# Anchors of a decay scan in one PSUM bank, early logits copied to SBUF, and a small product moved amid the value products: an attention and mixture-of-experts kernel on one core

## The chip, the cores and the metric

The kernel runs on one core of a Trainium2 chip. Five engines work side by side, each in its own order: TensorE (PE, matrix products), VectorE (DVE), ScalarE (ACT), GpSimd (POOL) and SyncE (SP), which here issues most of the transfers. Data lie in SBUF; PE writes to PSUM, which has eight banks of 512 float32 numbers for each of 128 partitions. The metric is the device time of one execution in microseconds, smaller being better.

## The reference

Three stages follow each other. The first is a linear attention with a decaying state, for 2 batches of 8 heads, 768 steps and 48 channels per head:

```python
for t in range(S):
    kt, vt, rt, wt = k[:, :, t], v[:, :, t], r[:, :, t], w[:, :, t]
    cur = einsum('bhd,bhe->bhde', u[None] * kt, vt)
    y[:, :, t] = einsum('bhd,bhde->bhe', rt, state + cur)
    state = wt[..., None] * state + einsum('bhd,bhe->bhde', kt, vt)
```

Its result, as 1536 tokens of 384 channels, goes through a mixture of 8 experts (the best expert by `x @ w_gate`, a capacity per expert, two matrices with a ReLU between them, the result scaled by the softmax weight), and then through a gated block with three matrices, `(silu(x @ w_gate) * (x @ w_val)) @ w_out`.

## The kernel before

The recurrence is done in 12 chunks of 128 steps, all heads at once. A chunk is split into two halves of 64 steps. The scan X (`prep1`, L369) forms the running products of the decay w in each half; `anchored` (L377) takes the reciprocals of X at every eighth step, the anchors; the scan R (`prep2`, L415) multiplies on from the anchors, step by step, with wm, which is w but zero where a group of eight begins (ACT fills wm in `prep0`, L406 and L407). X and R scale keys and queries: the products M (L421, L424). The data of a chunk come in as dm. The anchors stand in an SBUF tile anch of 526 columns, zero except for the 64 anchors; there are two such tiles, for even and odd chunks. `check` (L386) lets ACT sum up X and the anchors of a chunk, for a test of their size at the end.

PE then forms the products of a chunk: `scores` (`psA`, L469, copied out as A by ACT and masked by POOL), `kgtok` (transposed keys, `psT`), `state` (`psP`, L509 and L513, the state carried on, which DVE scales to Sc in L519 and ACT spreads to Sb in `expand`, L527), `values` (y, L494 and L499, in four pairs of heads) and `diag` (L441), the products with u. `xrow` (L533) adds to y the values weighted by the diagonal, aV, which POOL forms in `own` (L449). `gate_t` transposes x (L547), together with the diagonal's and the gate's rows (`gate_rows`), and ACT copies both out as xT (L552). `columns` (L576) turns these rows into columns with one matmul: the logits of the chunk before last, and the diagonal of the chunk to come, which ACT copies out as a8 (L578).

The loop `for u in range(NU - 2)` runs ten passes. Pass u prepares chunk u + 2 on DVE, forms the scores of chunk u + 1 and the values of chunk u. The order of every engine is the order in which the code is written (`manual_schedule`); `warm` puts matmuls whose result nobody reads on PE. The logits are taken in groups of chunks, (0 to 3), (4 to 7), (8, 9) and (10, 11). A group has one PSUM tile, of tag "lg" (but "P" for the third), for logits, diagonal and counts. `choose` writes the steps of a group's choice of experts into a list; `tick`, called between DVE's larger operations, takes the next from it. For the first group this happens in pass 6: one of the steps, taken between the two scans of `prep2(8)` and the products, is DVE's reciprocal of sm (L586) and, with it, ACT's scaling of four chunks, xg (L591). `count` (L652) and `place` (from L658) then give the tokens their places, and `scatter` writes them out.

PSUM is full: psA has two banks (A0, A1), psY two (y), and ps1 four, by tag: "T", "xT", "P" and "lg". A tile of a tag can be written only when all who use the tile before it in that bank have finished.

Of the kernel before, what the change touches and what calls it, by code (L numbers as in the profile page):

```python
# [10 lines left out]
F32 = mybir.dt.float32  # L11
# [14 lines left out]
HC = C // 2  # L26
# [3 lines left out]
G = 8  # L30
# [12 lines left out]
def build(tc, cap, dm, tk, vt, ub, cst, wg, w1, w2, wgate, wval, wout, out):  # L43
# [254 lines left out]
    early = ExitStack()  # L298
    ep = early.enter_context(tc.tile_pool(name="ep", bufs=2, side="right"))
    dmt = [ep.tile([128, DMW], F32, name=f"dm{i}", bufs=1) for i in range(3)]  # L300
    anch = [ep.tile([128, 2 * (NP * HC + G - 1)], F32, name=f"anch{i}", bufs=1) for i in range(2)]
    wm = [ep.tile([128, 2, NP, HC], F32, name=f"wm{i}", bufs=1) for i in range(2)]
    Sb = [ac.tile([128, NP, 2 * D], F32, name=f"Sb{i}") for i in range(2)]
    ap2 = at.enter_context(tc.tile_pool(name="ap2", bufs=2))
# [1 line left out]
    psA = at.enter_context(tc.tile_pool(name="psA", bufs=1, space=PSUM))  # L306
    ps1 = at.enter_context(tc.tile_pool(name="ps1", bufs=1, space=PSUM))
    psY = at.enter_context(tc.tile_pool(name="psY", bufs=2, space=PSUM))

    vts, Xf, Xt, Mt, kgt, Sc, At, yt, xt, xgt, xgs, av, rkt, a8s, lgt = ({} for _ in range(15))  # L310

    def run(x, up):

        x = x.rearrange("p a b -> p (a b)")
        return x if up else x[:, ::-1]

    def anchors(x, h, o):

        return x[:, h, :, h * o:h * o + HC - G + 1:G]

    def halved(x, w):
        return x[:, 0:2 * NP * w].rearrange("p (h a j) -> p h a j", h=2, a=NP)
# [1 line left out]
    def each8(x, w):  # L324


        return x.rearrange("p (h z) -> p h z", h=2)[:, :, 0:NP * w].rearrange("p h (a j) -> p h a j", a=NP)[..., 0:HC:G]
# [45 lines left out]
    def anchored(u):  # L373

        if u >= NU:
            return
        nc.vector.reciprocal(out=each8(anch[u % 2], HC), in_=each8(Xf[u], XW))  # L377
        tick()

    def check(u):  # L380

        if u >= NU:
            return
        for i, t in enumerate((each8(Xf[u], XW), each8(anch[u % 2], HC))):
            j = gp.tile([128, 2, NP, HC // G], F32, tag="sum", name="sum")
            nc.scalar.activation(out=j, in_=t, func=AF.Copy, accum_out=total[:, 2 * u + i:2 * u + i + 1])  # L386

# [21 lines left out]
    def prep2(u):  # L409

        if u >= NU:
            return
        Rt = ep.tile([128, 2, NP, HC], F32, tag="R", name="R")
        for h in range(2):
            nc.vector.tensor_tensor_scan(out=run(Rt[:, h], 1 - h), data0=run(wm[u % 2][:, h], 1 - h),  # L415
                                         data1=run(halved(anch[u % 2], HC)[:, h], 1 - h),
                                         initial=0.0, op0=ALU.mult, op1=ALU.add)
            tick()
        M = Mt[u] = ap3.tile([128, NP, 4, HC], F32, tag="M", name="M")
        kr = dmt[u % 3][:, 2 * NP * XW:].rearrange("p (a s j) -> p a s j", a=NP, s=4)  # L420
        nc.vector.tensor_tensor(out=M[:, :, 0::3, :], in0=kr[:, :, 0::3, :],  # L421
                                in1=Xt[u][:, :, :, 1:1 + HC].rearrange("p h a j -> p a h j"), op=ALU.mult)
        tick()
        nc.vector.tensor_tensor(out=M[:, :, 1:3, :], in0=kr[:, :, 1:3, :],  # L424
                                in1=Rt[:, ::-1].rearrange("p h a j -> p a h j"), op=ALU.mult)
        tick()
        if u < NU - 1:
            prep3(u)
# [23 lines left out]

    def warm(n, ps=None, tag="T"):

        ps = (ps or psA).tile([128, 512], F32, tag=tag if ps else "A0", name="psW")
        x = xinit.rearrange("p h a j -> p (h a j)").bitcast(BF16)[:, 0:512]
        for _ in range(n):
            nc.tensor.matmul(ps, ones, x, start=True, stop=True)

# [101 lines left out]

    def logits_to(u):
        g = group[u]
        if g not in lgt:
            lgt[g] = ps1.tile([128, len(g), 3 * E], F32, tag="P" if g[-1] == NU - 3 else "lg", name="lg")
        return lgt[g][:, u - g[0]]
# [6 lines left out]
    def columns(u, w, q):  # L573

        to = logits_to(w)
        nc.tensor.matmul(to[:, 0:2 * E], gss.pop(u), fold[:, 0:2 * E], start=True, stop=True)  # L576
        a8s[q] = gp.tile([128, H], F32, tag="a8", name="a8")
        nc.scalar.copy(out=a8s[q], in_=to[:, E:2 * E])  # L578

# [21 lines left out]
    def choose(us, weigh=weigh):  # L601

        n = len(us)
        u0, u1 = us[0], us[-1] + 1
        lg = lgt[us][:, :, 0:E]

        def over(x):
            return x.to_broadcast([128, n, E])

        mx, ls, ex, eq, be, sm = (small(t, n, w) for t, w in (  # L610
            ("mx", 1), ("ls", E), ("ex", E), ("eq", E), ("be", 1), ("sm", 1)))

        def s2():
            nc.vector.reduce_max(out=mx, in_=lg, axis=AX.X)

        def s3():
            nc.vector.tensor_tensor(out=ls, in0=lg, in1=over(mx), op=ALU.subtract)
            nc.scalar.activation(out=ex, in_=ls, func=AF.Exp)

        def s4():  # L620
            nc.vector.scalar_tensor_tensor(out=eq, in0=ls, scalar=0.0, in1=ev.unsqueeze(1).to_broadcast([128, n, E]),
                                           op0=ALU.is_ge, op1=ALU.mult)

        bes[us] = be

        def s5():
            nc.vector.reduce_max(out=be, in_=eq, axis=AX.X)

        def s6():
            nc.vector.tensor_tensor(out=ohs[:, u0:u1, :], in0=eq, in1=over(be), op=ALU.is_equal)  # L630

        def s7():
            nc.vector.reduce_sum(out=sm, in_=ex, axis=AX.X)

        w = weigh(us, sm)
        steps.extend([s2, s3, s4, s5, s6, s7, *w[:1], lambda: [f() for f in w[1:]]])
# [10 lines left out]
    def count(us):  # L647

        u0, n = us[0] // 4 * 4, len(us)
        pc = lgt[us][:, :, 2 * E:]  # L650
        adds = [(ohacc, us[0])] * (u0 > 0) + [(ohs[:, q, :], max(us[0], q + 1)) for q in range(u0, us[-1])]
        nc.tensor.matmul(pc, tri, ohs[:, us[0]:us[-1] + 1, :], start=True, stop=False, skip_group_check=True)  # L652
        for i, (o, q) in enumerate(adds):
            m = us[-1] + 1 - q
            nc.tensor.matmul(pc[:, n - m:], ones, o.unsqueeze(1).to_broadcast([128, m, E]), start=False,
                             stop=i == len(adds) - 1, skip_group_check=True)
# [201 lines left out]
    nc.vector.memset(xinit[:, 1, :, 1:2], 1.0)  # L858
    for i in range(2):
        nc.gpsimd.memset(wm[i], 0.0)  # L860
        nc.vector.memset(anch[i], 0.0)
    nc.vector.memset(ones, 1.0)
    prep0(0)
    prep1(0)
# [14 lines left out]
    prep1(1)  # L879
    anchored(1)  # L880
    prep2(1)
    prep0(2)
    prep1(2)
    for i in range(2):
# [3 lines left out]
    for u in range(NU - 2):  # L888
        chosen, counted = ended.get(u - 2), ended.get(u - 3)
        if u:  # L890
            prep0(u + 2)
            prep1(u + 2)
        xrow(u - 1)
        state(u)
        anchored(u + 2)
        warm((7, 4)[u] if u < 2 else 3, ps1, "xT")
        scores(u + 1)
        if u:
            own(u)
        kgtok(u + 1)  # L900
        if u:
            gate_t(u - 1, (u - 2 if u > 1 else None, u + 1))
        else:
            psr = ps1.tile([128, 2 * C], F32, tag="xT", name="psr")
            gs = gp.tile([128, DM + C], F32, tag="xT", name="gs", bufs=3)
            for q in range(2):
                diag(q, psr[:, C * q:C * q + C], True)
            nc.scalar.copy(out=gs[:, 0:2 * C], in_=psr)
            gss.update((q, gs[:, C * q:C * q + C]) for q in range(2))
            warm(2, ps1, "lg")  # L910
        expand(u)
        load_dm(u + 4)
        zero(NZ)
        if counted:
            count(counted)
            place(counted)
            ready += counted
        prep2(u + 2)
        if not u:
            check(1)  # L920
            nc.vector.tensor_copy(out=tri, in_=before)
        check(u + 2)
        if u:
            values(u)
            columns(u - 1, max(u - 2, 0), u + 1)
        else:
            values(u)
            for q in range(2):
                to = logits_to(q)
                nc.tensor.matmul(to[:, 0:E], gss.pop(q), fold[:, E:2 * E], start=True, stop=True)  # L930
            a8 = gp.tile([128, 2, H], F32, tag="a82", name="a82")
            nc.scalar.copy(out=a8, in_=lgt[group[0]][:, 0:2, 0:E])
            for q in range(2):
                a8s[q] = a8[:, q, :]
            own(0)
        if chosen:
            flush()
            if u < NU - 3:
                choose(chosen)
        load_v(u + 3)  # L940
        if u >= 4:
            load_raws(u - 3)
        if u >= 5:
            fill(0.0)
        for _ in range(2):
            if ready and not steps:
                scatter(ready.pop(0))
# [613 lines left out]
```

## Time and profile before

| | |
|---|---|
| time, median of 3 runs | 469.25 us (469.13 to 470.42) |
| time of the profiled execution | 465.57 us |
| its span, first to last instruction | 463.9 us |
| PE busy | 450.2 us (97%) |
| DVE busy | 331.0 us (71%) |
| ACT busy | 238.8 us (51%) |
| POOL busy | 70.9 us (15%) |
| mean granted clock of TensorE | 0.999 |
| recurrence and choice of experts | to about 97 us |

The span lies 1.7 us below the time of its own execution. Busy time of PE is modelled at the ends of matmuls, so a busy PE is not PE at its peak. Times in rows are counted from the span's start; an instruction's line is that of the kernel before.

### The profile page before, as it was taken

The numbers are of one execution on the slowest core, as the hardware profiler recorded it, in microseconds if no ns is written. First come the engines' busy times: TensorE is split into PE (matmuls) and PEld (weight loads), VectorE is DVE, ScalarE is ACT, GpSimd is POOL, SyncE is SP. The second block draws the span as 40 slices with busy tenths as digits, with TensorE's granted clock in tenths as the row PEclk, the third lists the DMA queues.
The fourth block names the chain that finished last, engine by engine and source line by source line (L and its number), as shares of the span: only waits on it lengthen the run. The fifth ranks groups of instructions, "written<-read, shape, count | busy, mean of one in ns | idle before, by whom it ended". The sixth has DMA issues, their size and how long they took to land.

```text
span 463.9 us, 9305 instructions
## 1 busy us (share of the span) xinstructions
PE 450.2 (97%) x3565; PEld 397.8 (86%) x3576; DVE 331.0 (71%) x690; ACT 238.8 (51%) x561; POOL 70.9 (15%) x94
## 2 busy tenths in 40 slices
PE   7998999999999999999999999999999999999994
PEld 3676767889999999999988888888888888888884
DVE  8999999877887945858599876665678585434241
ACT  4556685666877866674446454544443352231120
POOL 3324355540000000000000650000000000003033
PEclk9999999999999999999999999999999999999999
DMA  7798994139999944336134455222200000001011
GB/s 247 219 290 266 314 279 163 70 103 305 378 350 361 357 171 144 91 116 199 42 101 131 75 68 70 68 68 69 68 1 0 3 0 0 1 0 69 0 70 68
DMA packets 34801, 62.57 MB, mean 135 GB/s; under 512 B 5504, under 2 KB 17280, under 8 KB 34752
## 3 DMA queue, kind: packets, MB, share of 16 engines
q1 hardware_dynamic: 32832, 57.20, 40.5%
q0 software_dynamic: 1920, 4.73, 2.8%
q8 instruction: 29, 0.48, 0.5%
q14 instruction: 20, 0.16, 0.1%
HBM read 52.48 MB, written 9.44 MB: 133 GB/s over the span
## 4 chain that ended last, share of the span: by engine, by line
PE 80%; DVE 9%; issue 4%; DMA 4%; ACT 1%; POOL 1%; POOLq 0%; SPq 0%; DVEq 0%; ACTq 0%
PE psg L1418 32%; PE psu L1441 14%; PE psh L1297 14%; PE pso L1315 13%; DMA dm<-in_dm 2%; DVE R L415 2%; DVE X L369 2%; DVE M L424 1%; POOL out L1453 1%; PE psA L469 1%; PE y L494 1%; PE y L499 1%; PE psx L1282 1%; DVE rk L434 1%; DVE anch L377 1%
## 5 line engine op out<-in xcount | busy, mean ns | idle before, releaser
L1418 PE MATMUL psg<-yb,wu 128*128 128x512 f32 x648 | 156.3, 395 | 0.0
L1418 PEld LDWEIGHTS psg<-yb,wu 128*128 128x128 f32 x648 | 121.3, 188 | 26.2
L1441 PE MATMUL psu<-wu,a 128*128 128x384 f32 x432 | 80.8, 336 | 0.0
L1441 PEld LDWEIGHTS psu<-wu,a 128*128 128x128 f32 x432 | 76.4, 188 | 2.9
L1297 PE MATMUL psh<-xe,wu 128*128 128x240 f32 x576 | 69.1, 277 | 0.9 <-DVE xe L835 0.9
L1297 PEld LDWEIGHTS psh<-xe,wu 128*128 128x128 f32 x576 | 66.2, 190 | 1.2 <-DVE xe L835 1.1
L1315 PE MATMUL pso<-h,wu 128*128 128x240 f32 x576 | 66.4, 275 | 0.0
L1315 PEld LDWEIGHTS pso<-h,wu 128*128 128x128 f32 x576 | 65.4, 189 | 0.0
L1425 DVE TENSOR_TENSOR t<-t,psg 128x512 f32<-128x512 f32 x36 | 24.7, 686 | 51.9 <-PE psg L1418 38.9
L213 DVE TENSOR_TENSOR wu<-raw,wu 128x512 fp32r<-128x512 f32 x96 | 61.6, 684 | 0.0
L207 ACT CAST wu<-raw 128x512 fp32r<-128x512 f32 x96 | 54.9, 620 | 3.0 <-PE pso L1315 1.4
L1430 ACT CAST a<-t 128x512 fp32r<-128x512 f32 x36 | 22.3, 620 | 60.3 <-DVE t L1425 60.3
L1304 DVE SCALAR_TENSOR_TENSOR h<-psh,h 128x240 fp32r<-128x240 f32 x64 | 25.0, 403 | 23.2 <-ACT h L1303 22.9
L207 ACT CAST wu<-bits 128x384 fp32r<-128x384 f32 x36 | 18.0, 513 | 42.0 <-DVE bits L200 41.9
L1453 POOL DMA_INDIRECT out<-acc,idc x12 | 11.7, 975 | 173.6 <-DVE acc L1451 172.1
L1330 POOL DMA_INDIRECT idl<-ids,dests x12 | 13.5, 1124 | 159.0 <-DVE dests L795 155.6
L1424 ACT ACTIVATE t<-psg 128x512 f32<-128x512 f32 x36 | 21.5, 597 | 30.2 <-PE psg L1418 30.1
L1431 DVE TENSOR_TENSOR a<-t,a 128x512 fp32r<-128x512 f32 x36 | 24.8, 689 | 13.2 <-ACT a L1430 13.2
L1303 ACT ACTIVATE h<-psh 128x240 fp32r<-128x240 f32 x64 | 23.3, 374 | 9.8 <-PE psh L1297 9.1
L1451 DVE TENSOR_TENSOR acc<-psu,acc 128x384 f32<-128x384 f32 x24 | 12.9, 558 | 19.9 <-PE psu L1441 19.9
L471 ACT COPY A<-psA 128x512 f32<-128x512 f32 x24 | 12.8, 586 | 19.0 <-PE psA L469 19.0
L472 POOL TENSOR_SCALAR_AFFINE_SELECT A<-A 128x512 f32<-128x512 f32 x24 | 15.4, 665 | 43.6 <-ACT A L471 43.6
(156 smaller groups left out, 554.5 us busy)
## 6 DMA issues: line engine op xcount, KB each, us to landing
raw<-in_moe_w SPq DMA_DIRECT2D x32, 768.0 KB, 10.8
scr<-zrow SPq DMA_DIRECT2D x12, 384.0 KB, 4.9
raw<-in_moe_w_gate SPq DMA_DIRECT2D x6, 768.0 KB, 4.8
raw<-in_moe_w_val SPq DMA_DIRECT2D x6, 768.0 KB, 4.4
raw<-in_moe_w_out SPq DMA_DIRECT2D x6, 768.0 KB, 4.3
dm<-in_dm SPq DMA_DIRECT2D x18, 192.0 KB, 4.4
v<-in_tk SPq DMA_DIRECT2D x12, 192.0 KB, 6.5
dm<-in_dm SPq DMA_DIRECT2D x18, 99.0 KB, 4.7
```

What stands on the lines that cost most here:

```text
L207: nc.scalar.copy(out=slot_t[u % NSLOT][:, 0, c:c + n], in_=bits[i])
L213: nc.vector.tensor_tensor(out=w[:, 1, c:c + n], in0=bits.pop(i), in1=R(w[:, 0, c:c + n]), op=ALU.subtract)
L1297: nc.tensor.matmul(ps, w[:, a, k, c0:c0 + 128], xet[e][:, b, k, :], start=n == 0, stop=n == 8)
L1303: nc.scalar.activation(out=h[:, 0, :], in_=ps, func=AF.Relu)
L1304: nc.vector.scalar_tensor_tensor(out=h[:, 1, :], in0=ps, scalar=0.0, in1=R(h[:, 0, :]), op0=ALU.max, op1=ALU.subtract)
L1315: nc.tensor.matmul(ypt[e, d], w[:, a, f % 4, 128 * d:128 * d + 128], h[:, b, :], start=f == 0 and n == 0, stop=f == 7 and n == 2)
L1418: nc.tensor.matmul(gps[i][g], w[:, a, g, k, c0:c0 + 128], yb[t, k][:, c], start=a_ == k == 0, stop=a_ == k == 2)
L1424: nc.scalar.activation(out=t, in_=pg[0], func=AF.Silu)
L1425: nc.vector.tensor_tensor(out=t, in0=t, in1=pg[1], op=ALU.mult)
L1430: nc.scalar.copy(out=a[:, 0], in_=t)
L1431: nc.vector.tensor_tensor(out=a[:, 1], in0=t, in1=R(a[:, 0]), op=ALU.subtract)
L1441: nc.tensor.matmul(out_ps[t, j], att[i][:, c, 128 * j:128 * j + 128], w[:, a, f % 4, :], start=f % FP == 0 and n == 0, stop=f % FP == FP - ...
```

## The change

The two SBUF tiles anch become one PSUM tile of 512 columns, which holds the bank "lg" until the last chunk is prepared. The reciprocals are written into it, R's scans and ACT's check read it there. Since "lg" is taken, the logits of chunks 0 to 7 can't collect in it: `columns` writes logits and diagonal to a small tile of tag "P", and ACT copies all 16 columns to a row of lgs in SBUF, from which `choose` and `own` read. The counts of the first group take a tile of tag "P", those of the second one of tag "lg". From pass 1 on, `columns` stands between the first and the second half of the values, and `check` behind `columns`. In pass 0 the two diagonals go to a tile "P" too, the check of chunk 1 stands before the loop, and two warm matmuls write to a y tile, 384 columns wide. From pass 2 on there are two warm matmuls in place of three.

```diff
-    anch = [ep.tile([128, 2 * (NP * HC + G - 1)], F32, name=f"anch{i}", bufs=1) for i in range(2)]
...
+    anch = ps1.tile([128, 2 * NP * HC], F32, tag="lg", name="anch")
+    inv = anch.rearrange("p (h a j g) -> p h a j g", h=2, a=NP, g=G)[..., 0]
+    lgs = ac.tile([128, NU - 3, 2 * E], F32, name="lgs")
...
+    def turned(x, up):
+        return x if up else x[:, ::-1]
...
-        nc.vector.reciprocal(out=each8(anch[u % 2], HC), in_=each8(Xf[u], XW))
+        nc.vector.reciprocal(out=inv, in_=each8(Xf[u], XW))
...
-        for i, t in enumerate((each8(Xf[u], XW), each8(anch[u % 2], HC))):
+        for i, t in enumerate((each8(Xf[u], XW), inv)):
...
-                                         data1=run(halved(anch[u % 2], HC)[:, h], 1 - h),
+                                         data1=turned(anch[:, h * (NP * HC - G + 1):][:, 0:NP * HC], 1 - h),
...
+        w = DM if ps is psY else 512
+        ps = (ps or psA).tile([128, w], F32, tag=tag if ps else "A0", name="psW")
...
     def logits_to(u):
         g = group[u]
+        if g[-1] < NU - 4:
+            return ps1.tile([128, 2 * E], F32, tag="P", name="to")
...
         nc.tensor.matmul(to[:, 0:2 * E], gss.pop(u), fold[:, 0:2 * E], start=True, stop=True)
+        if w < NU - 4:
+            w = w if q == w + 3 else NU - 4
+            nc.scalar.copy(out=lgs[:, w, :], in_=to)
+            a8s[q] = lgs[:, w, E:]
+            return
...
-        lg = lgt[us][:, :, 0:E]
+        lg = lgs[:, u0:u1, 0:E] if u1 <= NU - 4 else lgt[us][:, :, 0:E]
...
+        if us[-1] < NU - 4:
+            lgt[us] = ps1.tile([128, n, 3 * E], F32, tag="P" if us[-1] < NU - 5 else "lg", name="lg")
         pc = lgt[us][:, :, 2 * E:]
...
     for i in range(2):
         nc.gpsimd.memset(wm[i], 0.0)
-        nc.vector.memset(anch[i], 0.0)
+    nc.vector.memset(anch, 0.0)
...
     prep2(1)
+    check(1)
...
-        warm((7, 4)[u] if u < 2 else 3, ps1, "xT")
+        warm((7, 4)[u] if u < 2 else 2, ps1, "xT")
...
-            warm(2, ps1, "lg")
+            warm(2, psY, "y")
...
         if not u:
-            check(1)
             nc.vector.tensor_copy(out=tri, in_=before)
-        check(u + 2)
         if u:
+            values(u, (0, 1))
+            columns(u - 1, max(u - 2, 0), u + 1)
+            check(u + 2)
+            values(u, (2, 3))
+        else:
+            check(u + 2)
             values(u)
-            columns(u - 1, max(u - 2, 0), u + 1)
-        else:
-            values(u)
+            to = ps1.tile([128, 2, E], F32, tag="P", name="to")
             for q in range(2):
-                to = logits_to(q)
-                nc.tensor.matmul(to[:, 0:E], gss.pop(q), fold[:, E:2 * E], start=True, stop=True)
+                nc.tensor.matmul(to[:, q], gss.pop(q), fold[:, E:2 * E], start=True, stop=True)
             a8 = gp.tile([128, 2, H], F32, tag="a82", name="a82")
-            nc.scalar.copy(out=a8, in_=lgt[group[0]][:, 0:2, 0:E])
+            nc.scalar.copy(out=a8, in_=to)
```

## Rows read from the trace of the kernel before

**Rows 1.** The chain of waits: start us, us, what.

```profile
36.77 1.25 DVE R L415
...
61.92 0.55 PE psx L547 x3
...
97.14 8.54 PE psh L1297 x72
```

**Rows 2.** Busy time of the engines by stretch, two passes.

```profile
core 0: us, PE busy (x) PEld busy (x) DVE busy (x) ACT busy (x) POOL busy (x), PEclk, DMA share, GB/s
33.11:39.67 6.56, 6.51 (x109) 5.02 (x109) 6.35 (x12) 4.20 (x13) 2.46 (x3) 1.00 0.82 257
51.90:59.27 7.37, 6.13 (x97) 4.53 (x97) 7.37 (x25) 5.13 (x14) 2.02 (x3) 1.00 1.06 289
```

**Rows 3.** PE's timeline, 45 to 62 us: start, us, what, [idle before, releaser].

```profile
45.75 1.16 PE L469 MATMUL psA<-M 64*128 64x128 f32 x16 [0.96 <-DVE M L424]
...
56.88 0.57 PE L509 MATMUL psP<-Sc,ident 128*128 128x192 f32 x2
57.38 0.67 PE L513 MATMUL psP<-v,kgt 128*64 128x48 f32 x16
...
59.27 1.16 PE L469 MATMUL psA<-M 64*128 64x128 f32 x16 [0.46 <-DVE M L424]
...
61.92 0.33 PE L547 MATMUL psx<-ident,x 128*128 128x128 f32 x1 [0.33 <-DVE x L533]
```

**Rows 4.** DVE's timeline, 5 to 60 us: scans of R.

```profile
5.76 1.27 DVE L415 TENSOR_TENSOR_SCAN R<-wm,anch 128x256 f32<-128x256 f32 x2
...
10.73 1.81 DVE L415 TENSOR_TENSOR_SCAN R<-wm,anch 128x256 f32<-128x256 f32 x2
...
23.29 1.86 DVE L415 TENSOR_TENSOR_SCAN R<-wm,anch 128x256 f32<-128x256 f32 x2
...
30.14 1.47 DVE L415 TENSOR_TENSOR_SCAN R<-wm,anch 128x256 f32<-128x256 f32 x2
...
36.16 1.86 DVE L415 TENSOR_TENSOR_SCAN R<-wm,anch 128x256 f32<-128x256 f32 x2
...
42.57 1.94 DVE L415 TENSOR_TENSOR_SCAN R<-wm,anch 128x256 f32<-128x256 f32 x2
...
48.53 2.06 DVE L415 TENSOR_TENSOR_SCAN R<-wm,anch 128x256 f32<-128x256 f32 x2
...
56.04 1.17 DVE L415 TENSOR_TENSOR_SCAN R<-wm,anch 128x256 f32<-128x256 f32 x1
```

**Rows 5.** POOL's timeline, 25 to 40 us.

```profile
29.65 0.83 POOL L449 TENSOR_TENSOR aV<-v,a 128x384 f32<-128x384 f32 x1
...
36.21 1.27 POOL L449 TENSOR_TENSOR aV<-v,a 128x384 f32<-128x384 f32 x1
```

**Rows 6.** Lines L516 and L519: ns min/median/max, first and last start us.

```profile
L516 DVE TENSOR_TENSOR d<-X x10: 133/150/580, 15.5 to 81.0; 128x4 f32<-128x4 f32 x10
...
L519 DVE TENSOR_TENSOR Sc<-psP,d x10: 358/358/359, 15.7 to 81.3; 128x192 f32<-128x192 f32 x10
```

**Rows 7.** The page's costliest groups: busy, mean ns of one, idle before.

```profile
L1425 DVE TENSOR_TENSOR t<-t,psg 128x512 f32<-128x512 f32 x36 | 24.7, 686 | 51.9 <-PE psg L1418 38.9
...
L213 DVE TENSOR_TENSOR wu<-raw,wu 128x512 fp32r<-128x512 f32 x96 | 61.6, 684 | 0.0
```

**Rows 8.** PE's timeline, 86 to 92 us: warm matmuls.

```profile
86.78 0.81 PE L458 MATMUL psW<-xinit,ones 128*128 128x512 bf16 x3
...
88.76 1.24 PE L458 MATMUL psW<-xinit,ones 128*128 128x512 bf16 x5
```

**Rows 9.** ACT's timeline, 55 to 62 us.

```profile
57.97 2.13 ACT L591 ACTIVATE xg<-x,sm 128x384 f32<-128x384 f32 x4 [1.40 <-DVE sm L586]
...
60.61 0.14 ACT L578 COPY a<-lg 128x8 f32<-128x8 f32 x1
```

**Rows 10.** All engines' timeline, 29 to 36 us.

```profile
31.76 0.67 PE L513 MATMUL psP<-v,kgt 128*64 128x48 f32 x16
...
35.24 0.36 DVE L519 TENSOR_TENSOR Sc<-psP,d 128x192 f32<-128x192 f32 x1
```

More of the change, by code (lines that the diff above doesn't have):

```diff
@@ L315, in run @@
         return x if up else x[:, ::-1]
-    def anchors(x, h, o):
-        return x[:, h, :, h * o:h * o + HC - G + 1:G]
+    def turned(x, up):
+        return x if up else x[:, ::-1]
     def halved(x, w):
@@ L453, in warm @@
     def warm(n, ps=None, tag="T"):
-        ps = (ps or psA).tile([128, 512], F32, tag=tag if ps else "A0", name="psW")
-        x = xinit.rearrange("p h a j -> p (h a j)").bitcast(BF16)[:, 0:512]
+        w = DM if ps is psY else 512
+        ps = (ps or psA).tile([128, w], F32, tag=tag if ps else "A0", name="psW")
+        x = xinit.rearrange("p h a j -> p (h a j)").bitcast(BF16)[:, 0:w]
         for _ in range(n):
```

## The prediction

> **What bounds the kernel now.** I read the chain of waits first, then the busy time by stretch, then each engine's timeline in the stretches that the change touches. From 97.14 us on the chain is almost one unbroken row of TensorE (PE) matmuls [rows 1]; nothing of the change lies there, so whatever the recurrence gains or loses before that point should pass through to the end, as its weights wait in buffers by then. In the recurrence (8 to 97 us) the chain lies on VectorE (DVE) first, in the scans of R, and on PE from about 62 us [rows 1]. The stretches say why: between one `psA` and the next (6.56 us) PE is busy 6.51 us and DVE 6.35 us, so the two are nearly balanced; in pass 6, from 51.90 us, DVE is busy all of 7.37 us and PE only 6.13 [rows 2]. PE's timeline shows who leads: at 45.75 and at 59.27 us `psA` waits for DVE's M [rows 3]. So until about 60 us DVE sets the pace, with PE some tenths of a microsecond behind, and after it PE. I number passes by the loop's u.
>
> **The scans of R.** Two scans take 1.27 us when POOL is quiet, at 5.76 us; later pairs take up to 2.06 [rows 4]. POOL's product aV explains it: from 36.21 it overlaps the pair that takes 1.86 us and itself takes 1.27 us, while at 29.65 it had half a microsecond to itself and took 0.83 [rows 5]. Both engines lose, and the chain shows the second scan of that pair alone at 1.25 us. An operation of DVE with two inputs in SBUF is thus held up while POOL reads SBUF: the 4-element product d takes from 133 to 580 ns. Sc, with one input in PSUM and one in SBUF, takes 358 to 359 ns in all ten passes, also amid POOL's masks [rows 6]. With the anchors in PSUM the scan has one input in SBUF (wm), as Sc has, so I expect 1.27 us for each pair. Of the pairs up to pass 6 the shown ones lose 0.54, 0.59, 0.20, 0.59, 0.67, 0.79 and (its first scan 1.17 against some 0.66, half of a quiet pair with the overlap) 0.51 us: 3.89 us in sum [rows 4]. The bounds are nothing and all of it; I take all, by Sc.
>
> Against that stands the price of PSUM itself. A 512-element product takes 686 ns with an input in PSUM and 684 with both in SBUF [rows 7]: reading costs nothing more. No row shows DVE writing PSUM, as the reciprocal now does. Below, that is nothing; above, I charge each reciprocal and each scan the 133 ns of a whole smallest operation [rows 6], 0.40 us a pass, 3.2 us over the eight pairs up to pass 6. I take zero, nearest to the rows of 512 elements. The Trainium skill (Perfetto Trace Analysis, Optimizing Scalar/DVE Operations) states about 125 ns of access for DVE on PSUM against 60 on SBUF. The rows of 512 elements do not show that difference. By the page, as an estimate, three operations in eight passes would lose 1.6 us, and the sum below would be about 468.8 us.
>
> **One anchor bank for two buffers.** The reciprocal of pass u+1 now waits for ScalarE's (ACT's) `check` of pass u, and that check waits for the scans. Three products, the two scans of X and three smaller operations of DVE lie between the R scans of one pass and the reciprocal of the next, and ACT needs only this check and one small copy in that time, so both waits cost nothing; behind the check ACT has only `prep0`, whose wm is read by the R scans of the next pass. One memset for two saves 0.5 us at the start, where DVE waits for the first load anyway.
>
> **The warm matmuls.** Three take 0.81 us and five 1.24, so one takes 0.215 [rows 8]. One goes in each of passes 2 to 9. PE gains that only where it sets the pace: passes 8 and 9 here, 0.43 us. In pass 0 two shrink from 512 to 384 columns: nothing that counts.
>
> **The diagonal's product amid the values.** The same matmul, moved ahead of half the values. It needs ACT's copy of xT, which ends about where the first half of the values ends; I take no wait. It costs PE nothing and frees ACT earlier. It issues no DMA.
>
> **The logits by way of bank P.** Here is the cost. The product of `columns` now goes to the tile "P" that `state` also uses, and a copy on ACT empties it. So PE's first matmul of `state(u+1)`, `psP`, must wait for that copy, and the copy stands in ACT's order behind all that was issued earlier. In most passes that is xT and `expand`: the copy is through about half a microsecond before PE has done the other half of the values, so no wait. In pass 6 it is not so. The ticks within `prep2` put the four scalings of xg on ACT, and these wait for DVE's reciprocal sm, which stands behind the R scans. ACT stood 1.40 us for it, ran the four from 57.97 in 2.13 us and copied the logits' neighbour only at 60.61 [rows 9]. PE had written `psP` at 56.88, long before that [rows 3], because it lay in another bank. Now it can't. Behind it on PE stand the warm matmuls and `psA` of chunk 8.
>
> New times of that place, on before's clock: DVE is 3.89 us earlier, so the scalings start at 54.08 and end at 56.21; the copy takes 0.15, and `psP` starts at 56.4. By before it takes 1.1 us to the end of `psP` [rows 3]; two warm matmuls with their issue take 0.5: `psA` at 58.0, against 59.27. **Gain there 1.27 us.** PE, without its stall of 0.96 us [rows 3] and with five warm matmuls less (1.07 us), would have been there 2 us before 56.88 or sooner; so it stands before `psP` for 1.5 to 2.5 us. What PE gains or loses in passes 0 to 5 (a short wait for the copy of a8 in pass 0 too) therefore goes into that wait.
>
> For this DVE must not wait for PE on the way. Its Sc reads `psP`: PE wrote it from 31.76, and DVE came to it at 35.24 [rows 10], so it has 2.8 us to run ahead, and the 2 us that PE itself comes earlier on top; the 3.89 us fit. M of chunk 8 is ready long before 58.0.
>
> After pass 6 PE sets the pace: its wait of 0.33 us for x at 61.92 [rows 3] goes, as DVE is ahead, and two warm matmuls: 0.43. **Sum: 1.27 + 0.33 + 0.43 = 2.0 us.** The tail until 87 us is PE after PE, then a chain of small steps and scatters that starts from it, all moved alike. Logits read from SBUF in the choosing cost as much as from PSUM. Loads of dm are issued two passes, some 12 us, ahead of their X scan, and land in less, so two microseconds earlier still find them there.
>
> The profiled execution took 465.57 us with a span of 463.9; the median of the runs is 469.25, 3.7 above it. I take the 2.0 us off both: 463.6 for a profile, **467.2 us** for the median. The three runs span 469.13 to 470.42; 0.3% (1.4 us) is about what a measurement can tell from no change.
>
> **The rivals.**
> 1. *No wait at bank P* (the copy on ACT gets there early enough, or the scalings come sooner): then `psA` of chunk 8 is bound by M (3.89 us earlier) or by PE itself (2 us or more); at 3 us, and with 0.33 and 0.43, the gain is 3.8 us: 465.5. For it speaks that PE has nothing else to wait for; against it the order on ACT, which the rows show plainly. Chance 0.12.
> 2. *The bank is dearer for DVE.* At half the upper price (1.6 us) the gain left is 0.4: 468.8; at the full price, 1.2 us slower: 470.4. The rule of the Trainium skill weighed above (Perfetto Trace Analysis) is this rival. Against it stand the 512-element rows; for it, that no row shows DVE writing PSUM. Chance 0.17.
> 3. *PE's clock falls in the gap before `psP`.* The longest wait that before shows here is 0.96 us, and the `psA` behind it took 1.16 us as everywhere [rows 3]; 1.5 to 2.5 us it does not show. At the lower of the two levels, 1.2 GHz, work takes twice as long, so 2 us of PE's work at it eat the whole gain: 469.2. Chance 0.07.
> 4. *Slower: the scans still stand behind aV.* Place: the R scans; price: the scalings stay at 57.97 to 60.10, the copy ends at 60.25, `psP` starts at 60.3, `psA` of chunk 8 at 61.9, which is 2.6 us later than before; 0.33 and 0.43 come back: 1.8 us slower, 471.1. It decides as soon as less than 1.8 of the 3.89 us come off the scans. For it: one input of the scan (wm) and its output remain in SBUF. Against it: Sc at 358 ns throughout. Chance 0.14.
>
> **How the numbers follow.** The forecast as summed has 0.50; its own range is 466.0 to 468.4 (the DVE gain wrong by a microsecond either way), 0.06 of it within 0.3% and 0.44 faster. Faster: 0.44 and rival 1, 0.12: 0.56. Same: 0.06, 0.14 of rival 2, 0.05 of rival 3, 0.02 of rival 4: 0.27. Slower: 0.03, 0.02 and 0.12: 0.17. The range runs from 464.9 (rival 1 at most of M's 3.89) to 469.9 (rivals 2 and 3 but for their ends); it leaves out rival 4 and little else, so it holds some 8 in 10.
>
> **What the profile of the changed kernel would show.** Right: scans of R at about 0.66 us each in every pass and aV at 0.83; PE idle 1.5 to 2.5 us before `psP` of state(7), released by ACT's copy to lgs, and that copy directly behind the four scalings; `psA` to `psA` at about 6.3 us in passes 8 and 9, with PE busy all through; the first `psh` some 2 us earlier. Wrong: pairs of R still above 1.8 us (rival 4), a reciprocal well above 0.55 us or scans above 0.66 (rival 2), matmuls behind the gap at twice their time (rival 3), no gap before that `psP` (rival 1). The forecast also falls if DVE begins to wait for ACT's check before the reciprocal, or for dm at an X scan.

## The result and the profile after

The changed kernel takes **472.56 us** (median of 4 runs, 471.71 to 473.22); before takes 469.19 us beside it (469.10 to 470.42). The ratio is 1.0065, with a 95% interval of 1.0040 to 1.0089: slower by 3.4 us, outside the predicted range. The profiled execution takes 472.21 us with a span of 470.5 and a mean granted clock of 0.986.

The busy time by stretch of the changed kernel, pass 3 first, then pass 6 up to `psA` of chunk 8, then this place and what follows it in smaller pieces:

```profile
core 0: us, PE busy (x) PEld busy (x) DVE busy (x) ACT busy (x) POOL busy (x), PEclk, DMA share, GB/s
33.01:39.59 6.58, 6.58 (x109) 5.08 (x108) 6.37 (x12) 4.09 (x13) 2.50 (x3) 1.00 0.80 254
50.49:60.91 10.42, 7.40 (x97) 5.24 (x96) 10.04 (x33) 7.73 (x23) 2.02 (x3) 0.86 1.05 294
55.40:58.00 2.60, 0.06 (x3) 0.02 (x1) 2.60 (x9) 2.26 (x6) 0.00 (x0) 0.99 1.05 202
58.00:60.90 2.90, 2.90 (x20) 1.54 (x20) 2.53 (x8) 0.99 (x6) 0.00 (x0) 0.50 1.07 270
60.90:64.60 3.70, 3.70 (x32) 3.08 (x34) 3.61 (x6) 1.52 (x3) 0.87 (x2) 0.50 1.08 231
64.60:69.20 4.60, 4.60 (x82) 3.32 (x73) 1.65 (x3) 2.57 (x11) 4.12 (x4) 0.98 0.79 221
```

Pass 3 takes 6.58 us, before 6.56 [rows 2]. The stretch that took 7.37 us before takes 10.42. In it PE stands almost idle from 55.4 to 58.0 us, and then works at a granted clock of 0.50, the lower of its two levels (1.2 GHz), until about 64.8. The timeline of PE, ACT and DVE in the changed kernel shows what it stood for:

```profile
54.76 0.67 PE L501 MATMUL y<-v,A 128*64 128x48 f32 x16
...
55.56 0.15 DVE L595 RECIPROCAL sm<-sm 128x4 f32<-128x4 f32 x1
...
55.74 2.13 ACT L600 ACTIVATE xg<-x,sm 128x384 f32<-128x384 f32 x4 [0.75 <-DVE sm L595]
...
57.77 0.15 ACT L583 COPY lgs<-to 128x16 f32<-128x16 f32 x1
...
57.98 1.01 PE L511 MATMUL psP<-Sc,ident 128*128 128x192 f32 x2 [2.54 <-ACT lgs L583]
...
58.92 1.10 PE L515 MATMUL psP<-v,kgt 128*64 128x48 f32 x16
...
59.95 1.03 PE L460 MATMUL psW<-xinit,ones 128*128 128x512 bf16 x2
...
60.91 2.08 PE L471 MATMUL psA<-M 64*128 64x128 f32 x16
```

`psP` waits 2.54 us for ACT's copy of the logits, which stands behind the four scalings of xg, and these behind DVE's reciprocal of sm. The two steps of `psP` take 1.01 and 1.10 us for 0.57 and 0.67, and `psA` takes 2.08 for 1.16 [rows 3]. `psA` of chunk 8 comes at 60.91 us (59.27 before), that of chunk 11 at 82.56 us in this trace and at 79.30 in that of before: 3.26 us late, nearly all of the 3.4 us by which the medians differ.

At `psh`, the first matmul of the experts, it is 6.62 us late (103.76 against 97.14 [rows 1]). The other 3.36 us are not the change's: the profiled execution of before in [rows 1 to 10] is an unusual one, 465.57 us where its runs take 469.25. A later profile of the same kernel before (469.18 us, span 467.5, clock 0.994) looks in the small steps of the tail as that of the changed kernel does. Its timeline of DVE and PE there:

```profile
90.88 0.17 DVE L709 TENSOR_TENSOR t<-lg,ohs 128x16 f32<-128x16 f32 x1 [2.38 <-remote]
...
92.47 0.17 PE L652 MATMUL lg<-ohs,tri 128*128 128x16 bf16 x1 [2.04 <-DVE ohs L630]
```

The same execution by stretch (columns as in [rows 2]), first from `psA` of chunk 11 to `psh`, then a part of it:

```profile
79.12:100.74 21.62, 18.44 (x208) 15.35 (x208) 15.60 (x65) 12.02 (x32) 10.59 (x17) 0.92 0.20 74
...
93.58:96.99 3.41, 3.41 (x11) 2.88 (x9) 3.27 (x14) 3.36 (x7) 1.51 (x4) 0.50 0.11 40
```

There DVE waits 2.38 us until 90.88 for a count whose last matmul stands at 88.49 us in the trace, then PE 2.04 us for DVE, and the clock falls. From `psA` of chunk 11 to `psh` this takes 21.62 us, in the changed kernel 21.20. So the place for which both kernels are compared is `psA` of chunk 11.

**The scans of R.** The timeline of DVE and POOL in pass 3 of the changed kernel:

```profile
34.88 1.26 DVE L416 TENSOR_TENSOR_SCAN R<-wm,anch 128x256 f32<-128x256 f32 x2
...
36.11 1.31 POOL L450 TENSOR_TENSOR aV<-v,lgs 128x384 f32<-128x384 f32 x1
...
36.65 1.32 DVE L425 TENSOR_TENSOR M<-dm,R 128x512 f32<-128x512 f32 x1
```

DVE's operations of the changed kernel from 5 to 83 us, grouped by line: busy us and mean ns of one, then the idle time ahead:

```profile
L370 DVE TENSOR_TENSOR_SCAN X<-dm,xinit 128x264 f32<-128x264 f32 x23 | 15.9, 725 | 0.0
L416 DVE TENSOR_TENSOR_SCAN R<-wm,anch 128x256 f32<-128x256 f32 x24 | 15.3, 674 | 1.0
L425 DVE TENSOR_TENSOR M<-dm,R 128x512 f32<-128x512 f32 x12 | 10.7, 894 | 0.0
...
L422 DVE TENSOR_TENSOR M<-dm,X 128x512 f32<-128x512 f32 x12 | 8.8, 736 | 0.0
L378 DVE RECIPROCAL anch<-X 128x64 f32<-128x64 f32 x12 | 6.7, 554 | 0.2
```

The same view of before:

```profile
L415 DVE TENSOR_TENSOR_SCAN R<-wm,anch 128x256 f32<-128x256 f32 x24 | 20.7, 899 | 1.0
L369 DVE TENSOR_TENSOR_SCAN X<-dm,xinit 128x264 f32<-128x264 f32 x23 | 15.1, 687 | 0.0
...
L424 DVE TENSOR_TENSOR M<-dm,R 128x512 f32<-128x512 f32 x12 | 8.1, 678 | 0.0
L421 DVE TENSOR_TENSOR M<-dm,X 128x512 f32<-128x512 f32 x12 | 8.1, 672 | 0.0
L377 DVE RECIPROCAL anch<-X 128x64 f32<-128x64 f32 x12 | 6.6, 547 | 0.1
```

The scans of R shed 5.4 us of busy time, and the pair that stood at 1.86 us in [rows 4] stands at 1.26. But aV, still 1.31 us long, now runs beside the product M that follows, which takes 1.32 us for 0.68: the two groups of M grow by 3.3 us and the scans of X by 0.8. What POOL costs DVE has mostly moved one operation on.

### The profile page after: what moved, and what is told of

It reads as the page before. It is cut to its first block, busy times and chain, and to the rows that moved or that the text cites. A ratio compares the mean times of both kernels' runs of the same rounds, so it can differ in the third digit from the quotient of the medians.

```text
span 470.5 us, 9293 instructions
## 1 busy us (share of the span) xinstructions
PE 454.4 (97%) x3568; PEld 400.8 (85%) x3568; DVE 328.6 (70%) x689; ACT 238.1 (51%) x561; POOL 70.7 (15%) x94
## 4 chain that ended last, share of the span: by engine, by line
PE 88%; DMA 3%; issue 2%; DVE 2%; ACT 2%; POOL 1%; POOLq 0%; SPq 0%; DVEq 0%
PE psg L1431 31%; PE psu L1454 14%; PE psh L1310 14%; PE pso L1328 13%; PE psA L471 3%; DMA dm<-in_dm 2%; PE y L496 2%; DMA raw<-in_moe_w 2%; PE psW L460 2%; PE y L501 1%; PE x L840 1%; PE psP L515 1%; POOL out L1466 1%; PE psP L511 1%; PE psx L549 1%
## 6 DMA issues: line engine op xcount, KB each, us to landing
raw<-in_moe_w SPq DMA_DIRECT2D x32, 768.0 KB, 10.7
```

## The experiments

The expectations stand as they were written before each run. Twelve experiments ran in three groups of four, each group beside runs of before. The median of before was 469.2 to 469.3 us in the first and third group, and 465.6 in the second, where the kernels that were profiled show no late signals in the tail. A time of the second group is therefore compared only with 465.6. Ratios are to the runs of before of the same group.

### Is the tail the change's?

**The kernel before, once more.** No edit.

> The kernel before, once more, for the clock and span of its usual executions. Of the 6.6 us by which the profile of the changed kernel is later at psh, 3.3 us lie ahead of psA of chunk 11 and 3.3 us in the small steps of the tail behind it, where PE's signals come late and its clock halves again. Theory: the late signals of the tail belong to the usual execution of either kernel and only the profiled execution of before lacked them; then runs at about 469.2 us show a mean clock near 0.992 and a span near 467.5. Rival: the tail's loss comes from the change; then runs of before show 0.999 whatever their time.

469.25 us (ratio 0.9999, 0.9988 to 1.0009); all ten runs show a clock of 0.991 to 0.995. `psA` of chunk 8 stands at 59.09 us, within 0.2 of [rows 3], that of chunk 11 at 79.12, and the tail is the late one shown above. The theory holds: the kernel before has the late signals too, in the execution that was profiled and, by time and clock, in the other nine.

**The changed kernel, once more.** No edit.

> The changed kernel once more, beside runs of before on the same chip. Before runs at 469.3 us where PE's signals come late in the tail and at 465.6 us where they don't, and the changed kernel was profiled only in the first case. Theory (the loss of the change ends at psA of chunk 11, the late signals have nothing to do with it): 3.3 us above the runs of before beside it, 468.9 if those are at 465.6, 472.6 if they are at 469.3. Rival (the half clock in pass 6 is what makes the signals late afterwards): 6.6 us above before where before has none.

472.59 us beside 469.19 (1.0054, 1.0030 to 1.0078): 3.4 us. `psP` waits 2.47 us for ACT's copy, `psA` takes 2.08 us behind it. Before stood at 469.2 in this group, so the case where it has no late signals was not met. Against the rival speak before itself and the next two kernels: their clock doesn't fall in the recurrence, and in the tail DVE still waits 1.93 and 1.95 us and PE 1.97 and 2.01 in those two. Three of the ten runs took 469.37 to 470.74 us at a mean clock of 0.991 to 0.993, the others 471.68 to 473.39 at 0.984 to 0.987. The difference in clock is what one stretch of 6.8 us at half clock makes in 470 us (0.007), so the clock perhaps does not fall in pass 6 in every execution. That is not shown: of these runs only one (473.02 us) was profiled, and the clock of the tail differs between executions as well.

### The wait at bank P and the clock

**Another bank for the product of `columns`:**

```diff
-            return ps1.tile([128, 2 * E], F32, tag="P", name="to")
+            return ps1.tile([128, 2 * E], F32, tag="T", name="to")
```

> The changed kernel with the small tile of columns in bank T in place of bank P, so that psP of state(7) needn't wait for ACT's copy; everything else as changed. Theory (the loss is the wait at bank P and the half clock behind it): psP at 55.5 instead of 57.98, no half clock before 90 us, psA of chunk 8 at about 57.1 and of chunk 11 at about 76.9 (5.6 us before the changed kernel's 82.56), median about 467. Rival (the loss lies in the split values, the anchors in PSUM or the warm matmuls): within 1 us of the changed kernel's 472.6.

467.04 us (0.9946, 0.9927 to 0.9965), 5.5 us less than the changed kernel. `psP` starts at 55.14, `psA` of chunk 8 at 56.83, of chunk 11 at 77.14, all at the full clock.

**The scalings behind the copy, bank P kept:**

```diff
-        steps.extend([s2, s3, s4, s5, s6, s7, *w[:1], lambda: [f() for f in w[1:]]])
+        steps.extend([s2, s3, s4, s5, s6, s7, *w[:1], lambda: rows_.extend(w[2:]) or w[1]()])
...
             check(u + 2)
+            while rows_:
+                rows_.pop(0)()
             values(u, (2, 3))
```

> The changed kernel with the four scalings of xg in pass 6 issued behind the copy of the logits on ACT, the bank left as it is. Theory: ACT's order is what makes psP wait; the copy to lgs ends at about 54.9, psP starts at about 55.5, psA of chunk 8 at 57.1, chunk 11 at 76.9, median about 467, as with the other bank. Rival (the bank itself or ACT's load makes the wait): psP still after 57 us, median above 471.

466.88 us (0.9947, 0.9931 to 0.9964). The timeline of this kernel:

```profile
54.67 0.17 ACT L583 COPY lgs<-to 128x16 f32<-128x16 f32 x1
...
55.16 0.59 PE L511 MATMUL psP<-Sc,ident 128*128 128x192 f32 x2
...
55.67 1.61 ACT L600 ACTIVATE xg<-x,sm 128x384 f32<-128x384 f32 x3
```

The copy ends 0.3 us before PE is done with the values, and nothing waits. Two different edits that only take away this one wait give the same time, so the wait and what it triggers cost 5.5 to 5.7 us. That is more than the 3.4 us by which the changed kernel is slower: without the wait the rest of the change gains 2.3 to 2.4 us.

**PE kept busy during the wait:**

```diff
             values(u, (2, 3))
+            if u == 6:
+                warm(11, ps1, "xT")
```

> The changed kernel with 11 more warm matmuls (2.4 us) behind the values of pass 6, which fill PE's wait; the wait itself stays. Theory with the clock as a part of its own: psP still at 58.0, but at the full clock, psA of chunk 8 at 59.4 instead of 60.9 and chunk 11 at about 79.6 instead of 82.6, median about 469.5. Rival (the wait alone is the loss): psA of chunk 11 no earlier than 82, median 472.6.

469.15 us (0.9986, 0.9970 to 1.0001): 3.4 us less than the changed kernel, level with the kernel before. PE's timeline:

```profile
55.17 2.55 PE L460 MATMUL psW<-xinit,ones 128*128 128x512 bf16 x11
57.71 0.59 PE L511 MATMUL psP<-Sc,ident 128*128 128x192 f32 x2
58.23 0.67 PE L515 MATMUL psP<-v,kgt 128*64 128x48 f32 x16
58.84 0.60 PE L460 MATMUL psW<-xinit,ones 128*128 128x512 bf16 x2
59.37 1.16 PE L471 MATMUL psA<-M 64*128 64x128 f32 x16
```

`psP` starts no earlier than 57.71 us, yet `psA` is there at 59.37 and runs in 1.16 us; from this `psP` to the next one it takes 6.57 us (to 64.28), in the changed kernel 9.59 (57.98 to 67.57). So the cost of the wait splits: 3.4 us by the clock (472.56 to 469.15), 2.3 us by the wait itself (469.15 to 466.88).

### The other parts, one by one

**The anchors in SBUF again,** in the kernel with bank T:

```diff
-    anch = ps1.tile([128, 2 * NP * HC], F32, tag="lg", name="anch")
+    anch = ep.tile([128, 2 * NP * HC], F32, name="anch", bufs=1)
```

> The kernel with columns' tile in bank T, and the anchors in one SBUF tile of 512 columns instead of the PSUM bank; nothing else differs. Theory (an input in PSUM frees the scans of POOL): pairs of R at 1.8 to 2.0 us again in passes where aV runs, psA of chunk 8 at 58.5 to 59.3 instead of 56.83, median about 469. Rival (the scans got faster because aV moved in time): pairs stay at 1.26 us and the median at 467.

466.12 us beside 465.62 (1.0011, 1.0001 to 1.0020). The scans of R and `psA` of chunk 6 in its timeline:

```profile
36.24 1.97 DVE L416 TENSOR_TENSOR_SCAN R<-wm,anch 128x256 f32<-128x256 f32 x2
...
42.77 2.02 DVE L416 TENSOR_TENSOR_SCAN R<-wm,anch 128x256 f32<-128x256 f32 x2
...
46.02 1.16 PE L471 MATMUL psA<-M 64*128 64x128 f32 x16 [1.03 <-DVE M L425]
```

The pairs take 1.7 to 2.1 us from 10.7 us on but for one (1.34), PE waits for M again, and `psA` of chunk 8 is at 59.48 us, 2.65 us later than with the bank. The bank is what frees the scans; without it the rest of the change is worth nothing. (The expected 469 went by a before at 469.2 us; here before is at 465.6.)

**`columns` behind all the values again,** in the kernel with bank T:

```diff
-            values(u, (0, 1))
-            columns(u - 1, max(u - 2, 0), u + 1)
             check(u + 2)
-            values(u, (2, 3))
+            values(u)
+            columns(u - 1, max(u - 2, 0), u + 1)
```

> The kernel with columns' tile in bank T, and columns put back behind all the values. In the changed kernel a pass from 69 us on takes 6.58 us although a warm matmul is gone, and the stretch from psx to psP takes 2.66 us against 2.45 before. Theory (the diagonal's product amid the values costs PE 0.21 us a pass, two more changes between kinds of matmul): psx to psP 2.45 us again, passes of 6.36 us where PE sets the pace, psA of chunk 11 some 0.4 to 0.6 us earlier than the 77.14 with the split, median about 466.5. Rival (the 0.21 us is something else, or DVE sets the pace): psA of chunk 11 within 0.1 us.

**462.04 us** beside 465.62 (0.9924, 0.9907 to 0.9940): 3.6 us faster than the kernel before, and no half clock stands in its recurrence. In PE's timeline of this kernel the stretch from `psx` to `psP` is 2.45 us:

```profile
65.12 0.55 PE L549 MATMUL psx<-ident,x 128*128 128x128 f32 x3
...
67.57 0.57 PE L511 MATMUL psP<-Sc,ident 128*128 128x192 f32 x2
```

The pass from 62.88 to 69.21 us takes 6.33, and `psA` of chunk 11 comes at 75.73, 1.1 to 1.4 us earlier than in the four kernels with the split and no wait (76.88 to 77.14): more than expected, because with the scans freed PE sets the pace ahead of pass 5 as well: from 26.17 to 32.50 us a pass takes 6.33 here, and 6.58 in the kernel with bank T and the split (26.37 to 32.95). At `psA` of chunk 8 the lead is 0.70 us already (56.13 against 56.83).

**The split alone in the kernel before:**

```diff
-            values(u)
+            values(u, (0, 1))
             columns(u - 1, max(u - 2, 0), u + 1)
+            values(u, (2, 3))
```

> The kernel before, with columns between the two halves of the values and nothing else changed. Theory (two more changes between kinds of matmul cost PE 0.21 us a pass, and PE sets the pace in passes 8 and 9): psx to psP 2.66 us instead of 2.45, 0.4 to 0.6 us slower than before. Rival (it costs nothing by itself, as the prediction took it): the same as before within 0.1 us.

470.39 us beside 469.19 (1.0017, 1.0003 to 1.0032). PE's timeline:

```profile
69.18 0.55 PE L547 MATMUL psx<-ident,x 128*128 128x128 f32 x3
...
71.85 0.59 PE L509 MATMUL psP<-Sc,ident 128*128 128x192 f32 x2
```

2.67 us from `psx` to `psP`, against 2.45 in the trace of before (68.47 to 70.92), and the pass 66.94 to 73.73 takes 6.79 for 6.56 [rows 2]. The theory holds for the 0.21 us; the loss is larger than expected. `psA` of chunk 11 comes at 80.49 us, 1.37 after the 79.12 of before, and 0.65 of that stands at `psA` of chunk 8 already (59.74 against 59.09): PE pays in early passes too (26.55 to 33.34: 6.79 us).

**One warm matmul less in the kernel before:**

```diff
-        warm((7, 4)[u] if u < 2 else 3, ps1, "xT")
+        warm((7, 4)[u] if u < 2 else 2, ps1, "xT")
```

> The kernel before, with two warm matmuls instead of three from pass 2 on and nothing else changed. By the prediction: 0.43 us faster than before, from passes 8 and 9 alone, since DVE leads ahead of them. Rival (one less lets PE stand longer and the clock fall): slower, with a half clock in the records.

468.15 us beside 469.19 (0.9983, 0.9970 to 0.9996). The pass from 65.69 to 72.04 us takes 6.35; `psA` of chunk 11 comes at 78.56, 0.56 us before that of the same kernel with three (79.12). The 0.43 us of the prediction are near it in size, but not from passes 8 and 9 alone: 0.24 us stand at `psA` of chunk 8 (58.85 against 59.09). The medians differ by 1.0 us, of which the interval leaves 0.2 to 1.4; where the rest beyond `psA` of chunk 11 comes from was not looked into.

**No warm matmuls from pass 2 on,** in the kernel with bank T and `columns` behind the values:

```diff
-        warm((7, 4)[u] if u < 2 else 2, ps1, "xT")
+        if u < 2:
+            warm((7, 4)[u], ps1, "xT")
```

> The kernel with columns' tile in bank T and columns behind all the values, without the two warm matmuls from pass 2 on. If PE sets the pace from pass 8 on: two passes by two matmuls of 0.215 us, 0.86 us less than the 3.6 us below before that the same kernel has with them, 4.4 us below before. Rival (DVE's M is the next to be waited for: psA of chunk 8 already waits 0.20 us for it): 3.6 us below before, PE idle instead. Third: PE idle so often that its clock falls, slower than that by a microsecond or more.

464.47 us beside 469.19 (0.9877, 0.9844 to 0.9910; 461.84 to 466.31 in four runs): 4.7 us below before, close to the first reading, but not by its way in the execution that was profiled, the slowest of the four (466.31 us). Its timeline of all engines in pass 6:

```profile
50.30 1.66 ACT L207 CAST wu<-raw 128x512 fp32r<-128x512 f32 x3 [2.52 <-DMA raw<-in_moe_w]
...
54.63 0.39 PE L580 MATMUL to<-fold,xT 128*128 128x16 f32 x2 [2.19 <-ACT xT L554]
```

ACT stands 2.52 us for weights that are still on their way, its copy of xT comes late, PE waits 2.19 us, and the clock falls behind it (0.56 from 56.52 to 60.00 us; one `psA` takes 2.08). In this execution the transfers of weights are the next limit.

### The tail, tried without result

**Five warm matmuls fewer, and nine more,** ahead of the last group's choice, in the kernel with late scalings:

```diff
-    warm(5, ps1, "T")
```
```diff
-    warm(5, ps1, "T")
+    warm(14, ps1, "T")
```

> The kernel with late scalings, without the five warm matmuls ahead of the last group's choice, in the stretch where DVE's product t waits 1.9 to 2.4 us for PE's count. Theory (PE is really behind its records there, and the signal comes when PE has worked off what was given to it): the signal and t come up to 1.1 us earlier. Rival (the signal is held for another reason): t at the same place, 88.8 us. The clock falls in either case; median 466 to 467.5.

> The kernel with late scalings, with 14 warm matmuls instead of five in that place (1.9 us more of PE). Theory (PE works off what it was given, the clock falls in the gap): the clock stays at its full level behind the gap, which gives back 1.4 us of the x products that follow; if the signal of the count waits for PE to be done, t comes up to 1.9 us later and nothing is won, else the median falls to about 465.5.

464.40 us (0.9970, 0.9960 to 0.9980) and 464.43 (0.9977, 0.9967 to 0.9986) beside 465.62 (with none, nine executions took 463.25 to 464.58 us, which the ratio is of, and one 1546.71). In this group the signals were prompt, so the theories of the late signals were not put to the test. With none, DVE doesn't wait, PE stands 1.10 us for ohs, and the clock is 0.50 from 88.5 to 91.9 us; with 14, the clock stays, but t waits 0.96 us for PE. From `psA` of chunk 11 to `psh` it takes 18.98 and 19.00 us, in the kernel with bank T and `columns` behind the values, which keeps five, 17.86: either edit makes the tail some 1.1 us longer. The kernel with late scalings did not run in this group with its five, so its median there is not known.

## Why the prediction was wrong

**The step that failed** is "psP at 56.4: psA at 58.0, against 59.27; gain there 1.27 us", in both of its halves: how late `psP` is, and how long the work behind it takes.

*How late `psP` is.* The place, the chain of causes and the length of PE's stand (2.54 us for "1.5 to 2.5") were right. But `psP` came at 57.98, 1.6 us later than forecast, as sm came at 55.56 us: 2.23 us before the 57.79 of before, and not 3.89. The prediction's own row, the pair of scans that overlaps aV [rows 5], shows two engines that hinder each other; freeing the scan left aV as it was, and it hit what DVE ran next. DVE's timeline of the changed kernel has the other operations that it hit up to then, besides the M of pass 3 shown above:

```profile
29.75 1.15 DVE L422 TENSOR_TENSOR M<-dm,X 128x512 f32<-128x512 f32 x1
...
43.18 1.31 DVE L425 TENSOR_TENSOR M<-dm,R 128x512 f32<-128x512 f32 x1
...
54.30 0.75 DVE L592 TENSOR_SCALAR sm<-sm 128x4 f32<-128x4 f32 x1
```

Against the same operations of before:

```profile
31.53 0.66 DVE L421 TENSOR_TENSOR M<-dm,X 128x512 f32<-128x512 f32 x1
...
57.13 0.14 DVE L583 TENSOR_SCALAR sm<-sm 128x4 f32<-128x4 f32 x1
...
57.79 0.14 DVE L586 RECIPROCAL sm<-sm 128x4 f32<-128x4 f32 x1
```

The three M and this step give back 0.49, 0.64, 0.63 and 0.61 us, 2.4 us of the 3.89 that the scans did gain; each of them overlaps an aV (from 29.53, 36.11, 42.68 and 54.19 us). Smaller operations that were longer before, ohs and d, return some 0.8, which leaves the 2.23. The Trainium skill (SBUF — State Buffer, section "SBUF: two separate sides") states that a VectorE operation with two SBUF inputs and a GpSimd operation that reads SBUF exclude each other. The trace agrees for scans and products alike: 0.68 us became 1.32 beside an aV of 1.31. So the term should have been the scans' gain less what the next operations take over. With the clock kept, this step gives about nothing: `psA` of chunk 8 at 59.37 us, against 59.09 in the usual profile of before; with the clock as it was, `psA` came at 60.91 and not at 58.0.

*What the gap triggers.* The sum took `psP` to `psA` at the full clock, 1.6 us; it took 2.93, and the half clock went on behind it. This is rival 3, to which 0.07 was given with a price of 2.0 us, for 2 us of work at half clock. It came, held for 6.8 us, and cost 3.4. Its argument was that the longest wait shown before, 0.96 us, left `psA` at 1.16; but the forecast itself had PE stand for up to 2.5 us, for which no row spoke.

The other steps:
- *Scans at 1.27 us with the anchors in PSUM*: right, 1.26 to 1.27 in every pair, and shown by the kernel with the anchors in SBUF. Rival 4 fell in its place, though a weaker form of it came true: POOL kept a part of the gain. aV, forecast at 0.83 us, took 1.21 to 1.31 in six of ten passes.
- *PSUM costs DVE nothing*: right. The reciprocal takes 554 ns writing PSUM and 547 writing SBUF, and Sc stays at 358. Rival 2 fell. The 125 against 60 ns of the Trainium skill (Perfetto Trace Analysis, Optimizing Scalar/DVE Operations) do not show in these rows: the reciprocal differs by 7 ns, and the measurement decides here.
- *One anchor bank for two buffers*: right. The idle time ahead of the scans of R is 1.0 us in both kernels, and that ahead of the reciprocals 0.1 before and 0.2 after.
- *The warm matmuls, 0.43 us*: about right in size by itself (0.56 us at `psA` of chunk 11 in the kernel before), though not from passes 8 and 9 alone.
- *The diagonal's product amid the values costs PE nothing*: wrong. Instead of following the last value product once, it stands between two groups of them, and PE pays 0.21 us a pass, which eats the warm matmuls' gain: the pass from 69.23 to 75.81 us takes 6.58 us, before 6.56. "Takes no wait" failed once too, by 0.47 us in pass 6.
- *The wait for x goes*: right by luck. `psx` has none behind the gap, as PE comes late there; in the kernels with bank T and with late scalings, where PE comes on time, it waits 0.34 and 0.28 us for x again.
- *The tail moves alike*: right within 0.4 us against the usual execution of before (21.62 and 21.20 us), wrong against the one of [rows 1 to 10] (17.84).

Without the wait the mechanism that the prediction trusted, faster scans, gives a gain as rival 1 said, if a smaller one: 2.3 us with the other bank (rival 1 had 3.8), 3.6 with `columns` behind the values as well.

## What to carry to other kernels

A tile that moves into a bank already in use takes over the order of every engine that empties it: ask what else that engine has queued ahead, and move that work (here four scalings) or the tile, before costing anything. Where a forecast contains a new gap of TensorE longer than those that the trace shows, a half clock behind it deserves more than a small chance, and a price for as long as it may hold (here 6.8 us). When one operation is freed from an engine that hindered it, look at what runs beside that engine next: the collision moves on.

## What the runs showed of the hardware

- Gaps of TensorE of 2.54 and 2.19 us in the recurrence, and of 2.04 and 1.10 in the tail, were followed by stretches at a clock of 0.50, of 3.4 us or 6.8 us (the latter in the changed kernel); gaps of 0.96 and 1.03 ahead of `psA` were not, nor was one of 1.69 us at 8.29 us in the kernel with the anchors in SBUF. So the length of the gap alone does not tell which way it goes.
- The two matmuls of `columns` amid the values lengthen PE's row by 0.21 us, though the instructions are the same. In the changed kernel 0.32 us pass from the start of the last values to that of `columns`, 0.32 from there to the next values and 0.31 from the last values to `psP`; in that of before 0.32 and 0.24, and 0.22 between the two halves of the values; within the second half the first step grows from 0.18 to 0.22.
- In one and the same kernel DVE got PE's finished count 2.2 us after its modelled end in one execution (469.18 us), and at once in another (465.57 us). The late count makes DVE and then PE wait, and the clock falls. By their times, the other runs of before fall mostly to the one kind in two groups and to the other in the third. What delays the count, the signal or PE itself behind its modelled times, is open.
